# Second half-batch's scores one and a half steps later, and score products behind a whole first projection

## The chip, the cores and the metric

The kernel runs on one core of one Trainium2 chip. The time is that of one execution on the device, in microseconds, from its first instruction to its last; several runs are taken and the median is compared. Before the change it is 1001.44 us, the median of three runs from 995.87 to 1004.9.

## The reference

Three stages follow one another. All arithmetic is float32.

```python
# q, k, v: (4 batches, 8 heads, 576 positions, 64)
q_d, k_d, v_d = means over 4 neighbouring positions          # 144 positions
out_up    = repeat(softmax(q_d k_d^T / 8) v_d, 4)            # coarse attention
out_local = softmax(q k^T / 8 where |i - j| < 4) v           # band attention
x = (out_up + out_local), heads side by side                 # (2304, 512)
h = x @ w_in;  y = (h * cos(h)) @ w_out                      # 512 -> 2048 -> 512
z = ((y @ w_a) * (y @ w_b)) @ w_out2                         # 512 -> 1536 -> 512
```

## The kernel before, in words

**Attention units.** Attention is done in eight units, each half of one batch (288 positions, all 8 heads as 4 pairs). For each pair hp, `local_scores` (line 199) multiplies q and k in five windows of 64 positions, two heads each: ten products of 64x64 into one PSUM tile, which DVE reads with the mask added, reduces to a maximum (line 223) and subtracts (line 224). `down_scores` (line 226) does the coarse scores: two products of 72x144 (line 235), each reduced by DVE (line 237) and copied by ACT (line 238). All PSUM tiles of attention share the tag `att`, which has two buffers. `exps` (line 243) then does the exponentials of a unit, behind an ACT table load, and normalising, transposes, the products with v (`attend`), `combine` and the splits of x into a high and a low part (`xsplit_hi`, `xsplit_lo`) follow.

**First network.** A float32 product is made of three float32r products: high x high, high x low, low x high (`mm3`, line 420). A step g of the first network takes one block of tokens and one 128-wide slice f of the 2048: `h_mm` (line 434) is the first projection, 4 x 3 = 12 products of 128x288 into a PSUM tile with tag `h`, two buffers. `cos_a` and `cos_b` compute h*cos(h): ACT reads h (line 460), DVE reduces it (line 461), ACT takes a sine (line 465) and a square (line 468), and a last DVE instruction (line 469) multiplies with h and sets the `h` tile free. `split_hi` and `split_lo` split the result, and `back_mm` of step g - 3 does the second projection, 12 products again. Blocks 0 and 1 hold 288 tokens each and go in four runs of eight steps: block 0 with slices 0 to 7, block 1 with the same, block 0 with slices 8 to 15, block 1 with these. Block 1 needs unit 1's output, so from step 8 on.

**Weights.** Weights come by DMA as raw 64-bit words through the queue of SP and are converted: two ACT instructions (lines 104 and 107) and one of DVE (line 109) make a float32, ACT writes the high part (line 116) and POOL the low part (line 117). Two slices are wanted per step at first, so beside each step ACT also does six such instructions.

**What sets the order.** Unit 0's attention stands alone at the start. Units 1 to 7 are threaded through the steps of the first network: `unit_slots(u, g0, gl)` (line 363) spreads the tasks of unit u, each with a due time from table `T` (`T1` for unit 1), over gl steps from step g0. Slot 2g is issued in the program behind `h_mm` of step g, slot 2g+1 behind the `back_mm` of that step. For unit 1 this is `unit_slots(1, 0, FS * C["S1"])` (line 552), from step 0 over 5.6 steps; unit 2 starts at step 14. The program's order is not the engines' order: a scheduler of the framework sees priorities and dependencies and puts instructions on each engine ahead of one another where it thinks them ready, and each engine then runs its list strictly in that order. `after(ins, earlier)` (line 92) adds a dependency that only holds the order in that list and makes no semaphore wait.

In the text, a step is a step g of the first network, counted from 0.

Of the kernel before, what the change touches and what calls it, by code (L numbers as in the profile page):

```python
# [20 lines left out]
NT, DM = B * S, H * D  # L21
# [12 lines left out]
SD = S // 4  # L34
# [4 lines left out]
STARTS = ((0, 57, 114, 171, 228), (285, 342, 399, 456, 512))  # L39
BASE = (0, 284)  # L40

C = {'AHEAD': 8, 'LEAD': 4, 'NPRE': 4, 'ND': 'ddd', 'XL': 'dpp', 'SUMS0': 'dddd', 'SUMS1': 'pppp', 'GLO': 8, 'FS': 8, 'S1': 0.7, 'G2': 14, 'LC': 0, 'DM': 2, 'LAG': 3, 'NGS': 3, 'MK': 0, 'SB': 'ddd', 'NL': 'dpp', 'W0': 0, 'W1': 0, 'W2': 0, 'W3': 0, 'NWV': 3, 'NGH': 4, 'XB': 8, 'YE': 6, 'CA': 2, 'CV': 1.0, 'NE': 26, 'RA': 5, 'SA': 6, 'SD': 3, 'PA': 1, 'LAG2': 2, 'PK': 1.0, 'GE': 'ad', 'NXF': 3, 'LP': 0, 'T': {'sums': [0, 0.5, 1.0, 3.0], 'ls': [0, 0, 0, 1.5], 'ds': [1, 1.5, 3, 4], 'ex': 6, 'ln': [6.0, 9.5], 'dn': [6, 7, 9, 10], 'dt': [7, 9.5, 11, 12], 'lt': [7.5, 8.5, 12.0, 13.5], 'at': [9.5, 9.5, 13.5, 14.5], 'xh': [11.0, 12.0, 15.0, 15.5], 'xl': [12.5, 13.5, 15.5, 15.5]}, 'T1': {'sums': [0, 0, 1.0, 2.0], 'ls': [0.5, 1.5, 2.5, 3.5], 'ds': [1, 1.5, 3, 4], 'ex': 5, 'ln': [5.5, 8], 'dn': [5.0, 6.0, 8.0, 9.0], 'dt': [6.0, 7.5, 10.0, 11.0], 'lt': [7.0, 8.0, 12.0, 12.0], 'at': [9, 9, 13, 14], 'xh': [9.0, 10.0, 13.0, 14.0], 'xl': [9.5, 11, 15, 15]}}


def window_cols(half):
# [13 lines left out]
def kernel(ctx, tc, qT, kT, vw, vds, w_in, w_out, w_a, w_b, w_out2, out):  # L59
# [21 lines left out]
    def att_ps(u):  # L81
# [3 lines left out]
        turn[0] += 1  # L85
        return ps.tile([128, 512], F32, tag=tag, name="att", bufs=1 if tag.startswith("acc") else 2)

    marks = []
    gate, h_ins = {}, {}
    slots = {}  # L90

    def after(ins, earlier):
        if earlier is not None:
            tc.add_manual_dep(ins.ins, earlier.name,
                              mybir.DependencyInfo(mybir.DependencyClass.NoSync, mybir.DependencyReason.DATA),
                              reason="paces the loads")
# [102 lines left out]
    def local_scores(u, hp):  # L199
        b, half = divmod(u, 2)  # L200
        p = att_ps(u)
        pem = u < C["MK"]
        if pem:
            pe.matmul(p[:, :NW * W].rearrange("p (w k) -> p w k", k=W), identb, maskb.unsqueeze(1).to_broadcast([128, NW, W]), start=True, stop=False)
        for w, (off, _, _, _) in enumerate(window_cols(half)):
            for a in range(2):
                r = slice(64 * a, 64 * a + 64)
                pe.matmul(
                    p[r, W * w:W * w + W],
                    qt[u, hp][r, off:off + W],  # L210
                    kt[b, hp][r, BASE[half] + off:BASE[half] + off + W],
                    start=not pem, stop=True,
                )
        if hp % 2 == 0:
            smx[u, hp // 2] = at.tile([128, NW, 2, W], F32, tag="smx", name="smx", bufs=2)
        sm = smx[u, hp // 2][:, :, hp % 2]
        src = p[:, :NW * W].rearrange("p (w k) -> p w k", k=W)
        if not pem:
            dve.tensor_tensor(out=sm, in0=src, in1=mask.unsqueeze(1).to_broadcast([128, NW, W]), op=ALU.add)
            src = sm  # L220
        mx = at.tile([128, NW], F32, tag="mx", name="mx", bufs=2)
        smr[u, hp] = mx
        dve.tensor_reduce(out=mx, in_=src, axis=AX.X, op=ALU.max)
        last["sub"] = (dve if pem else pick("SB", u)).tensor_tensor(out=sm, in0=src, in1=mx.unsqueeze(2).to_broadcast([128, NW, W]), op=ALU.subtract).ins

    def down_scores(u, hp):
        b, half = divmod(u, 2)
        if hp == 0:
            smd4[u] = at.tile([QD, HP, 2, SD], F32, tag="smd", name="smd", bufs=1)
        sm = smd4[u][:, hp]  # L230
        mx = at.tile([QD, 2], F32, tag="mxd", name="mxd", bufs=2)
        p = [att_ps(u) for a in range(2)]
        for a in range(2):
            r = slice(64 * a, 64 * a + 64)
            pe.matmul(p[a][:QD, :SD], qd[u, hp][r, :], kd[b, hp][r, :], start=True, stop=True)
        for a in range(2):
            dve.tensor_reduce(out=mx[:, a:a + 1], in_=p[a][:QD, :SD], axis=AX.X, op=ALU.max)
            last["neg"] = act.activation(out=sm[:, a], in_=p[a][:QD, :SD], func=AF.Identity, bias=mx[:, a:a + 1], scale=-1.0).ins
        smd[u, hp] = sm
# [123 lines left out]
    def unit_slots(u, g0, gl):  # L363
        T = C["T"] if u > 1 else C["T1"]
        todo = []
        for hp in range(HP):
            todo += [(T["sums"][hp], down_sums, u, hp), (T["ls"][hp], local_scores, u, hp), (T["ds"][hp], down_scores, u, hp),
                     (T["dn"][hp], down_norm, u, hp), (T["dt"][hp], down_transpose, u, hp),
                     (T["at"][hp], attend, u, hp), (T["at"][hp], combine, u, hp), (T["xh"][hp], xsplit_hi, u, hp),
                     (T["xl"][hp], xsplit_lo, u, hp, pick("XL", u))]  # L370
        todo += [(T["ex"], exps, u)]
        for pr in range(HP // 2):
            todo += [(T["ln"][pr], local_norm, u, pr)] + [(T["lt"][2 * pr + i], local_transpose, u, pr, i) for i in range(2)]
        todo += [(min(T['ls'][0], T['sums'][0]) + 1, load_q, u, 3)]
        for hp in range(HP):
            todo += [(6 + hp, load_k, u + 1, hp)] + ([(6 + hp, load_q, u + 1, hp)] if hp < 3 else [])
        todo += [(15, load_v, u + 1)]
        for i in range(H):
            todo += [(i, load_vs, u, i // 2, i % 2), (i + 2, sum_vs, u, i // 2, i % 2)]
        order = [load_vs, sum_vs, load_q, load_k, down_sums, local_scores, down_scores, exps, local_norm, down_norm, local_transpose,  # L380
                 down_transpose, attend, combine, xsplit_hi, xsplit_lo, load_v]
        for t, *task in sorted(todo, key=lambda t: order.index(t[1])):
            slots.setdefault(int(2 * (g0 + t / NF * gl)), []).append(task)
# [36 lines left out]
    def mm3(ps_out, lh, ll, rh, rl, start, stop):  # L420
        i = pe.matmul(ps_out, lh, rh, start=start, stop=False)  # L421
        pe.matmul(ps_out, lh, rl, start=False, stop=False)  # L422
        pe.matmul(ps_out, ll, rh, start=False, stop=stop)  # L423
        return i

    def proj(psum, whi, wlo, u):
# [7 lines left out]
    def h_mm(g, u, f):  # L434
        hps[g] = ps.tile([128, UN1[u][1]], F32, tag="h", name="h", bufs=2)
        ins = proj(hps[g], *wts["i", f], u)
        gate.setdefault(u + 1, ins)
        h_ins[g] = ins

    def back_mm(first, last, whi, wlo, hi, lo, n=NB):  # L440
# [64 lines left out]
    if True:  # L505
# [43 lines left out]
        seq = [(i, u, f) for i, (u, f0, f1) in enumerate(blocks) for f in range(f0, f1)]  # L549
        NG = len(seq)  # L550
        slots.clear()
        unit_slots(1, 0, FS * C["S1"])
        unit_slots(2, C["G2"], 2 * NF - C["G2"])
        for u in range(3, 7):
            unit_slots(u, 2 * NF + 12 * (u - 3), 12)
# [423 lines left out]
```

## Time and profile before

| | us |
|---|---|
| three runs, median (lowest to highest) | 1001.44 (995.87 to 1004.9) |
| span of the profiled execution | 1001.5 |
| PE busy in it | 964.9 |
| DVE busy | 669.1 |
| ACT busy | 581.9 |
| POOL busy | 327.9 |

The span of the profiled execution is its own time; it differs from the median of the runs by 0.06 us. PE is TensorE, DVE VectorE, ACT ScalarE, POOL GpSimd and SP the engine that issues the DMAs. Busy time of PE is counted at whatever clock was granted at the moment: 1.2 GHz shows as a granted clock of 0.50, 2.4 GHz as 1.00, and numbers between are stretches that hold both. A PE that is busy at 0.50 does half of the work per microsecond. Instructions of the profile carry lines of the kernel before; in the changed kernel the same instructions have line numbers 1 to 4 higher.

### The profile page before, as it was taken

What the parts mean: (1) busy time and instruction counts of PE and PEld (TensorE: products, weight loads), DVE (VectorE), ACT (ScalarE), POOL (GpSimd) and SP (SyncE); (2) the same over time, 40 slices, a digit from 0 to 9 for tenths busy, and PEclk for the clock granted to TensorE, in tenths of its full rate; (3) what the DMA queues carried; (4) which work ended last, traced back from release to release, by engine and by line L of the source; (5) the groups of instructions that cost most, each with busy time, mean ns of one, the idle gap of its engine ahead of it and who ended that gap; (6) DMA issues with size and microseconds to landing.
All of it is one profiled execution on the core that took longest, in us unless ns stands there. A gap on an engine that the chain in (4) does not pass through costs nothing. (4 is left out here: it accounts for less than half of the span.)

```text
span 1001.5 us, 18883 instructions
## 1 busy us (share of the span) xinstructions
PE 964.9 (96%) x6936; PEld 917.0 (92%) x6936; DVE 669.1 (67%) x1410; ACT 581.9 (58%) x1327; POOL 327.9 (33%) x463
## 2 busy tenths in 40 slices
PE   4999999999999999999998999999999999999998
PEld 3778888989889989899997999999999999999998
DVE  7567677577777867765456567676677667676752
ACT  5589897476776848676576743444444345434321
POOL 3756752014221441101045234442043330233310
PEclk8569999999999999999999999999999999999999
DMA  8546611144555363333277983326702128734000
GB/s 277 209 137 204 196 64 32 56 141 125 167 159 165 123 183 109 115 98 103 77 240 266 333 271 97 105 70 212 250 23 63 44 82 302 225 127 129 1 32 32
DMA packets 75644, 141.28 MB, mean 141 GB/s; under 512 B 6432, under 2 KB 46624, under 8 KB 75552
## 3 DMA queue, kind: packets, MB, share of 16 engines
q1 hardware_dynamic: 75552, 140.08, 42.9%
q8 instruction: 55, 0.90, 0.4%
q14 instruction: 37, 0.30, 0.1%
HBM read 110.95 MB, written 29.10 MB: 140 GB/s over the span
## 5 line engine op out<-in xcount | busy, mean ns | idle before, releaser
L832 DVE TENSOR_TENSOR ev<-ev,z 128x384 f32<-128x384 f32 x252 | 135.4, 550 | 70.9 <-PE z L423 67.6
L421 PE MATMUL h<-xh,w 128*128 128x288 f32 (+1 forms) x448 | 148.8, 332 | 8.7 <-DVE gs L469 8.7
L421 PE MATMUL acc<-gh,w 128*128 128x288 f32 (+1 forms) x448 | 144.8, 324 | 3.0 <-DVE ev L454 1.7
L422 PE MATMUL h<-xl,w 128*128 128x288 f32 (+1 forms) x448 | 145.3, 324 | 0.0
L422 PE MATMUL acc<-gl,w 128*128 128x288 f32 (+1 forms) x448 | 142.7, 319 | 1.6 <-POOL gl L477 1.4
L423 PE MATMUL h<-xh,w 128*128 128x288 f32 (+1 forms) x448 | 144.0, 321 | 0.0
L423 PE MATMUL acc<-gh,w 128*128 128x288 f32 (+1 forms) x448 | 142.1, 317 | 0.0
L790 POOL TENSOR_TENSOR sb<-w,sb 128x256 fp32r<-128x256 f32 x96 | 75.5, 787 | 186.3 <-ACT sb L788 169.4
L421 PEld LDWEIGHTS h<-xh,w 128*128 128x128 f32 x448 | 87.2, 195 | 16.7 <-DVE gs L469 12.2
L788 ACT ACTIVATE sb<-w 128x256 fp32r<-128x256 f32 x144 | 59.9, 416 | 66.2 <-PE z L423 62.5
L422 PE MATMUL z<-xl,sb 128*128 128x384 f32 x288 | 97.0, 337 | 0.0
L421 PE MATMUL acc<-gh,wb 128*128 128x384 f32 x288 | 96.9, 337 | 0.0
L423 PE MATMUL acc<-gh,wb 128*128 128x384 f32 x288 | 96.9, 337 | 0.0
L423 PE MATMUL z<-xh,sb 128*128 128x384 f32 x288 | 96.9, 336 | 0.0
L421 PE MATMUL z<-xh,sb 128*128 128x384 f32 x288 | 96.9, 336 | 0.0
L422 PE MATMUL acc<-gl,wb 128*128 128x384 f32 x288 | 96.9, 336 | 0.0
L421 PEld LDWEIGHTS acc<-gh,w 128*128 128x128 f32 x448 | 84.8, 190 | 9.1 <-issue 2.9
L469 DVE SCALAR_TENSOR_TENSOR gs<-gs,h 128x288 f32<-128x288 f32 (+1 forms) x112 | 55.2, 493 | 56.6 <-ACT gs L468 56.3
L422 PEld LDWEIGHTS h<-xl,w 128*128 128x128 f32 x448 | 87.7, 196 | 2.3 <-issue 0.9
L790 POOL TENSOR_TENSOR sb<-ws,sb 128x256 fp32r<-128x256 f32 x72 | 54.0, 749 | 108.4 <-ACT sb L788 84.8
L423 PEld LDWEIGHTS h<-xh,w 128*128 128x128 f32 x448 | 87.8, 196 | 1.5 <-issue 0.2
L422 PEld LDWEIGHTS acc<-gl,w 128*128 128x128 f32 x448 | 85.3, 190 | 3.5 <-POOL gl L477 1.6
(138 smaller groups left out, 2302.3 us busy)
## 6 DMA issues: line engine op xcount, KB each, us to landing
wb<-wd SPq DMA_DIRECT2D x72, 512.0 KB
raw<-in_w_in_dram SPq DMA_DIRECT2D x16, 512.0 KB
raw<-in_w_out_dram SPq DMA_DIRECT2D x16, 512.0 KB
praw<-in_w_a_dram SPq DMA_DIRECT2D x12, 512.0 KB
praw<-in_w_b_dram SPq DMA_DIRECT2D x12, 512.0 KB
praw<-in_w_out_dram SPq DMA_DIRECT2D x12, 512.0 KB
wd<-praw SPq DMA_DIRECT2D x12, 512.0 KB
wd_a<-praw SPq DMA_DIRECT2D x12, 448.0 KB
```

The source lines that it names most:

```text
L421: i = pe.matmul(ps_out, lh, rh, start=start, stop=False)
L422: pe.matmul(ps_out, lh, rl, start=False, stop=False)
L423: pe.matmul(ps_out, ll, rh, start=False, stop=stop)
L469: dve.scalar_tensor_tensor(out=s, in0=s, scalar=1.0, in1=hps[g], op0=ALU.subtract, op1=ALU.mult, reverse0=True)
L788: act.activation(out=t[:, 0], in_=blk, func=AF.Copy)
L790: (dve if nst[0] % C["SD"] == 0 else pool).tensor_tensor(out=t[:, 1], in0=blk, in1=t[:, 0].bitcast(F32), op=ALU.subtract)
L832: dve.tensor_tensor(out=dst, in0=a, in1=z, op=ALU.add)
```

## The change

Two things. A start `G1` of 1.5 replaces the 0 of unit 1's slots, so that all tasks of unit 1, not only its scores, are issued one and a half steps later. And every score product, local or coarse, of any unit that is issued after the first `h_mm`, is ordered on PE behind the last product of the latest `h_mm` that was issued before it: `mm3` notes its last product, `h_mm` keeps it. A score product can no longer slip in between the twelve products of the step it is issued behind, nor ahead of them. (It can still stand among the products of a later step.)

```diff
-C = {'AHEAD': 8, 'LEAD': 4, 'NPRE': 4, ...
+C = {'G1': 1.5, 'AHEAD': 8, 'LEAD': 4, 'NPRE': 4, ...
...
+    dense = {}
     marks = []
...
             for a in range(2):
                 r = slice(64 * a, 64 * a + 64)
-                pe.matmul(
+                ins = pe.matmul(
                     p[r, W * w:W * w + W],
...
+                after(ins, dense.get("h"))
...
-            pe.matmul(p[a][:QD, :SD], qd[u, hp][r, :], kd[b, hp][r, :], start=True, stop=True)
+            ins = pe.matmul(p[a][:QD, :SD], qd[u, hp][r, :], kd[b, hp][r, :], start=True, stop=True)
+            after(ins, dense.get("h"))
...
-        pe.matmul(ps_out, ll, rh, start=False, stop=stop)
+        dense["last"] = pe.matmul(ps_out, ll, rh, start=False, stop=stop).ins
...
         gate.setdefault(u + 1, ins)
+        dense["h"] = dense["last"]
...
-        unit_slots(1, 0, FS * C["S1"])
+        unit_slots(1, C["G1"], FS * C["S1"])
```

No instruction is added or left out; the lists of the engines are put in another order, from the first projection to about step 27. The first place is PE at steps 0 and 1. In the names, `h_530` is the PSUM tile of step 0, `h_549` or `h_633` that of step 1, `h_628` that of step 2; `att<-k,q` are local and `att<-kd,qd` coarse score products of unit 1; x10 is ten products in a row. Before:

```order
L421 MATMUL h_530<-xh_393,w_476 128x288
L422 MATMUL h_530<-xl_395,w_476 128x288
L423 MATMUL h_530<-xh_393,w_476 128x288
L208 MATMUL att_560<-k_101,q_320 64x64 x3
L421 MATMUL h_530<-xh_436,w_476 128x288
L208 MATMUL att_560<-k_101,q_320 64x64 x7
L235 MATMUL att_578<-kd_153,qd_548 72x144
L422 MATMUL h_530<-xl_438,w_476 128x288
L423 MATMUL h_530<-xh_436,w_476 128x288
L421 MATMUL h_530<-xh_468,w_476 128x288
L422 MATMUL h_530<-xl_470,w_476 128x288
```

And in the changed kernel, from the middle of step 1:

```order
L424 MATMUL h_549<-xh_393,w_484 128x288
L425 MATMUL h_549<-xl_395,w_484 128x288
L426 MATMUL h_549<-xh_393,w_484 128x288
L424 MATMUL h_549<-xh_436,w_484 128x288
L425 MATMUL h_549<-xl_438,w_484 128x288
L426 MATMUL h_549<-xh_436,w_484 128x288
L424 MATMUL h_549<-xh_468,w_484 128x288
L425 MATMUL h_549<-xl_470,w_484 128x288
L426 MATMUL h_549<-xh_468,w_484 128x288
L209 MATMUL att_602<-k_101,q_320 64x64 x10
L237 MATMUL att_620<-kd_153,qd_590 72x144
L237 MATMUL att_621<-kd_153,qd_590 72x144
```

Before, the first ten local products are cut in two by step 0, and pairs 0, 1 and 2 of unit 1 have their scores among the products of steps 0 to 2. After the change the 24 products of steps 0 and 1 stand in one row, pair 0 stands behind them, pairs 1 and 2 behind step 2, and pair 3 behind step 3.

The second place is POOL at the same time, where `w_484` is the low part of the first projection's weights of step 1 and `qd` are sums of q for the coarse scores of unit 1. Before:

```order
L183 TENSOR_TENSOR qd_552<-q_363 128x72
L184 TENSOR_TENSOR qd_552<-qd_552,q_363 128x72
L185 TENSOR_TENSOR qd_552<-qd_552,q_363 128x72
L183 TENSOR_TENSOR qd_556<-q_397 128x72
L117 TENSOR_TENSOR w_484<-raw_111,w_484 128x512
```

After:

```order
L184 TENSOR_TENSOR qd_594<-q_363 128x72
L185 TENSOR_TENSOR qd_594<-qd_594,q_363 128x72
L186 TENSOR_TENSOR qd_594<-qd_594,q_363 128x72
L118 TENSOR_TENSOR w_484<-raw_111,w_484 128x512
L118 TENSOR_TENSOR w_492<-raw_117,w_492 128x512
```

The weights' low part now stands ahead of the third pair's sum, which can only be written when the coarse products of pair 0 have let go of one of the two `qd` buffers.

The third place is PE again, where the scores of unit 2 stand. Before, three pairs together at once behind the back projection of step 5:

```order
L421 MATMUL acc<-gh,w 128x288
L422 MATMUL acc<-gl,w 128x288
L423 MATMUL acc<-gh,w 128x288
L208 MATMUL att<-k,q 64x64 x30
L235 MATMUL att<-kd,qd 72x144
L421 MATMUL h<-xh,w 128x288
```

After, behind the first projection of step 14, where they are issued:

```order
L425 MATMUL h<-xl,w 128x288
L426 MATMUL h<-xh,w 128x288
L209 MATMUL att<-k,q 64x64 x20
L424 MATMUL acc<-gh,w 128x288
L425 MATMUL acc<-gl,w 128x288
L426 MATMUL acc<-gh,w 128x288
L209 MATMUL att<-k,q 64x64 x10
L424 MATMUL acc<-gh,w 128x288
```

The scheduler had pulled the first three pairs of unit 2 some seven steps ahead of their slot; the order dependency now keeps them behind step 14, together with the coarse products and, from step 16, the fourth pair, which stood there before too.

## Rows read from the trace of the kernel before

**Rows 1.** The page's 40 slices of the span: granted clock of TensorE, in tenths.

```profile
PEclk8569999999999999999999999999999999999999
```

**Rows 2.** Stretches: length, then busy us of each engine (instructions), clock, DMA share, GB/s.

```profile
36.00:63.00 27.00, 27.00 (x154) 20.65 (x151) 15.84 (x35) 17.36 (x35) 11.81 (x17) 0.50 0.55 183
75.00:110.00 35.00, 30.87 (x291) 28.84 (x291) 24.43 (x44) 31.83 (x71) 25.43 (x26) 0.93 0.57 192
110.00:165.00 55.00, 50.50 (x393) 46.78 (x392) 42.29 (x90) 49.58 (x112) 28.52 (x33) 1.00 0.28 90
```

**Rows 3.** Stretches of 2 us, PE alone: busy us (products), clock, DMA share, GB/s.

```profile
62.00:64.00 2.00, 2.00 (x12) 0.72 0.16 66
98.00:100.00 2.00, 2.00 (x10) 0.50 0.75 185
```

**Rows 4.** Timeline of PE, from step 0 on; a score product shows as two instructions.

```profile
36.05 0.61 PE L421 MATMUL h<-xh,w 128*128 128x288 f32 x1
...
41.55 0.44 PE L422 MATMUL h<-xl,w 128*128 128x288 f32 x1
41.79 0.44 PE L423 MATMUL h<-xh,w 128*128 128x288 f32 x1
...
46.38 1.33 PE L208 MATMUL att<-k,q 64*64 64x64 f32 x20
47.65 0.75 PE L235 MATMUL att<-kd,qd 64*72 64x144 f32 x2
...
49.45 0.44 PE L423 MATMUL h<-xh,w 128*128 128x288 f32 x1
...
50.50 0.61 PE L421 MATMUL h<-xh,w 128*128 128x288 f32 x1
...
60.41 0.44 PE L421 MATMUL h<-xh,w 128*128 128x288 f32 x1
...
84.85 0.29 PE L421 MATMUL h<-xh,w 128*128 128x288 f32 x1
...
86.43 0.30 PE L421 MATMUL acc<-gh,w 128*128 128x288 f32 x1
```

**Rows 5.** Timeline of ACT; in brackets its idle time before, and what ended it.

```profile
39.11 0.64 ACT L116 ACTIVATE w<-raw 128x512 fp32r<-128x512 f32 x1
42.27 0.41 ACT L460 ACTIVATE gs<-h 128x288 int32<-128x288 f32 x1 [2.51 <-PE h L423]
...
46.56 0.43 ACT L468 ACTIVATE gs<-gs 128x288 f32<-128x288 f32 x1
49.93 0.41 ACT L460 ACTIVATE gs<-h 128x288 int32<-128x288 f32 x1 [2.93 <-PE h L423]
...
60.59 1.28 ACT L246 ACT_TABLE_LOAD   x1
```

**Rows 6.** Who ACT waited for, 36 to 63 us: total us, times, longest us.

```profile
ACT gs L460 <- PE h L423: 5.4, 2, 2.9
ACT smd L238 <- DVE mxd L237: 3.8, 4, 1.0
```

**Rows 7.** Timeline of DVE, where it works on step 0 and pair 0.

```profile
37.97 1.18 DVE L361 TENSOR_TENSOR xl<-xf,xh 128x288 fp32r<-128x288 f32 x2
40.09 0.49 DVE L219 TENSOR_TENSOR smx<-att,mask 128x320 f32<-128x320 f32 x1 [0.94 <-PE att L208]
40.77 0.30 DVE L237 TENSOR_REDUCE mxd<-att 72x1 f32<-72x144 f32 x1 [0.19 <-PE att L235]
...
49.74 0.44 DVE L469 SCALAR_TENSOR_TENSOR gs<-gs,h 128x288 f32<-128x288 f32 x1
```

**Rows 8.** Timeline of POOL at the same place.

```profile
43.27 1.30 POOL L117 TENSOR_TENSOR w<-raw,w 128x512 fp32r<-128x512 f32 x1
```

**Rows 9.** Timeline of PE behind unit 2's scores, and DVE's subtractions, 86 to 130 us (count, busy, mean ns).

```profile
96.79 0.40 PE L421 MATMUL h<-xh,w 128*128 128x288 f32 x1 [2.14 <-DVE gs L469]
...
L224 DVE TENSOR_TENSOR smx<-smx,mx 128x320 f32<-128x320 f32 x4 | 3.0, 760 | 0.0
```

More of the change, by code (lines that the diff above doesn't have):

```diff
@@ L40 @@
 BASE = (0, 284)
-C = {'AHEAD': 8, 'LEAD': 4, 'NPRE': 4, 'ND': 'ddd', 'XL': 'dpp', 'SUMS0': 'dddd', 'SUMS1': 'pppp', 'GLO': 8, 'FS': 8, 'S1': 0.7, 'G2': 14, 'LC': 0, 'DM': 2, 'LAG': 3, 'NGS': 3, 'MK': 0, 'SB': 'ddd', 'NL': 'dpp', 'W0': 0, 'W1': 0, 'W2': 0, 'W3': 0, 'NWV': 3, 'NGH': 4, 'XB': 8, 'YE': 6, 'CA': 2, 'CV': 1.0, 'NE': 26, 'RA': 5, 'SA': 6, 'SD': 3, 'PA': 1, 'LAG2': 2, 'PK': 1.0, 'GE': 'ad', 'NXF': 3, 'LP': 0, 'T': {'sums': [0, 0.5, 1.0, 3.0], 'ls': [0, 0, 0, 1.5], 'ds': [1, 1.5, 3, 4], 'ex': 6, 'ln': [6.0, 9.5], 'dn': [6, 7, 9, 10], 'dt': [7, 9.5, 11, 12], 'lt': [7.5, 8.5, 12.0, 13.5], 'at': [9.5, 9.5, 13.5, 14.5], 'xh': [11.0, 12.0, 15.0, 15.5], 'xl': [12.5, 13.5, 15.5, 15.5]}, 'T1': {'sums': [0, 0, 1.0, 2.0], 'ls': [0.5, 1.5, 2.5, 3.5], 'ds': [1, 1.5, 3, 4], 'ex': 5, 'ln': [5.5, 8], 'dn': [5.0, 6.0, 8.0, 9.0], 'dt': [6.0, 7.5, 10.0, 11.0], 'lt': [7.0, 8.0, 12.0, 12.0], 'at': [9, 9, 13, 14], 'xh': [9.0, 10.0, 13.0, 14.0], 'xl': [9.5, 11, 15, 15]}}
+C = {'G1': 1.5, 'AHEAD': 8, 'LEAD': 4, 'NPRE': 4, 'ND': 'ddd', 'XL': 'dpp', 'SUMS0': 'dddd', 'SUMS1': 'pppp', 'GLO': 8, 'FS': 8, 'S1': 0.7, 'G2': 14, 'LC': 0, 'DM': 2, 'LAG': 3, 'NGS': 3, 'MK': 0, 'SB': 'ddd', 'NL': 'dpp', 'W0': 0, 'W1': 0, 'W2': 0, 'W3': 0, 'NWV': 3, 'NGH': 4, 'XB': 8, 'YE': 6, 'CA': 2, 'CV': 1.0, 'NE': 26, 'RA': 5, 'SA': 6, 'SD': 3, 'PA': 1, 'LAG2': 2, 'PK': 1.0, 'GE': 'ad', 'NXF': 3, 'LP': 0, 'T': {'sums': [0, 0.5, 1.0, 3.0], 'ls': [0, 0, 0, 1.5], 'ds': [1, 1.5, 3, 4], 'ex': 6, 'ln': [6.0, 9.5], 'dn': [6, 7, 9, 10], 'dt': [7, 9.5, 11, 12], 'lt': [7.5, 8.5, 12.0, 13.5], 'at': [9.5, 9.5, 13.5, 14.5], 'xh': [11.0, 12.0, 15.0, 15.5], 'xl': [12.5, 13.5, 15.5, 15.5]}, 'T1': {'sums': [0, 0, 1.0, 2.0], 'ls': [0.5, 1.5, 2.5, 3.5], 'ds': [1, 1.5, 3, 4], 'ex': 5, 'ln': [5.5, 8], 'dn': [5.0, 6.0, 8.0, 9.0], 'dt': [6.0, 7.5, 10.0, 11.0], 'lt': [7.0, 8.0, 12.0, 12.0], 'at': [9, 9, 13, 14], 'xh': [9.0, 10.0, 13.0, 14.0], 'xl': [9.5, 11, 15, 15]}}
 def window_cols(half):
```

## Prediction

> **What bounds the kernel now.** I read the page's slices first. TensorE has the full clock nearly everywhere; it lacks it at the start, in the first three slices of 25 us [rows 1]. So the stretches come next. From 36 us, where the first projection begins, to 63 us PE is busy for 27.00 of 27.00 us at a granted clock of 0.50, the 1.2 GHz level; ACT is busy for 17.36 of them, so ACT has 9.64 us free [rows 2]. From 75 to 165 us it is otherwise: PE is busy for 30.87 of 35 and 50.50 of 55 us at 0.93 and 1.00, and ACT for 31.83 and 49.58 [rows 2]. There both are near 90% and wait for one another in turns; neither has much to give. So in the first stretch a slow PE is the bound and ACT is kept waiting, and in the second ACT's conversions of weights and cosines weigh as much as PE's products. ACT's own waits from 36 to 63 us say so: 5.4 us in two waits for the products of a step, 3.8 us in four waits for the maxima of coarse scores, which in their turn wait for PE [rows 6].
>
> When does the clock rise? In the stretch from 62 to 64 us (0.72, so the rise is inside it) [rows 3], after the twelve products of a step that starts at 60.41 with no attention between [rows 4]. In the 24 us before, the score products of unit 1 stood among the steps, PE was as busy, and the clock stayed at 0.50.
>
> A rule of the Trainium skill bears on this: "TensorE: Matmul & The Clock Gate", Part 1, says that the chip sets this clock by how busy the PE has recently been. By busy time alone it should have risen at once; the rows above speak against so simple a reading, and if it held, the clock of the changed kernel would gain nothing from the new order (the second rival).
>
> **The change, step by step.** Nothing is added or taken away, so the cost is in who waits for whom. Products of a step start 0.24 us apart at half clock (41.55 to 41.79), so twelve take 2.88 us; at full clock twelve take 1.58 (84.85 to 86.43) [rows 4]. Ten local products take 1.33 us at half clock, one coarse product 0.75 [rows 4].
>
> *Step 0.* It starts at 36.05 as before. The low parts of x for its last two groups come from DVE at about 38.6 and 39.15 (37.97 plus 1.18 for two) [rows 7], so half of it waits there: six products to 37.5, two waits, the last one at about 39.6 to 39.85. Before, it ended at 42.23 (41.79 plus 0.44) [rows 4], as 30 score instructions stood in it. ACT reads it at 39.85 and not at 42.27 [rows 5]: **2.4 us** of waiting gone.
>
> *Step 1.* The high part of its weights is ready at 39.75 (39.11 plus 0.64) [rows 5]. The low part was made by POOL at 43.27, in 1.30 us [rows 8], behind a sum that waited for a buffer; now it stands ahead of that sum, so from 39.75 to 41.05. PE loses about 0.8 us there and then does ten products: step 1 ends at 43.5, not at 49.9 (49.45 plus 0.44) [rows 4]. ACT's second long wait, 2.93 us [rows 5], goes: its list puts the read of step 1 behind the square of step 0, and that square moves from 46.56 to about 43.5 with the read. **2.9 us**.
>
> *Scores of pair 0 and step 2.* The ten local products go from 43.6 to 44.9 and the two coarse ones to 46.3, if the clock is still low. On DVE the last instruction of step 0's cosine, which sets the `h` tile free, now stands behind the maxima of pair 0: 46.3 plus 0.30 for the maximum and 0.44 for itself gives 47.05 [rows 7]. Step 2 starts there; before at 50.50 [rows 4], so 3.4 us sooner, with 0.75 us of idle PE. ACT's split of step 0 waits for the same DVE instruction: ACT is through with the weights ahead of it at about 44.7, so a **new wait of 2.35 us** (0.9 if the clock has risen by 43.5, as pair 0's products then take half).
>
> *Clock.* From 36.05 to 43.5 there are 24 products with two gaps of about 0.8 to 0.95 us, and no attention. That is twice the row of 60.41 to 63, so I expect 1.00 somewhere from 40 to 47 us, not at 63. From then on a step is 1.58 us, and ACT finds every step, and nearly all coarse maxima, ready. I leave 1.0 us of the 3.8 us of waits for maxima.
>
> *Exponentials.* Pair 3's scores end no later than before, since steps 2 and 3 run at full clock; the table load for them, at 60.59 before [rows 5], comes 0 to 1.5 us sooner. But steps 3 and 4 have then been read and more weights converted, which before came after it. During the exponentials PE runs dry, as it did before, and I expect the clock to fall once there too.
>
> *Queues.* On SP two more loads of weights stand ahead of the load of pair 3's q, which waits for pair 0's scores; weights come sooner, and q is needed only at step 3. Nothing there ends last.
>
> *Sum.* 2.4 + 2.9 + 3.8 - 1.0 - 2.35 = 5.75 us of ACT's time, out of 9.64 that were free; with the early rise inside step 1 it is 7.2. As ACT and PE are both near 90% up to 165 us, what ACT has gained at 63 us is carried to the end: I take **6.5 us**, between the two. The least is 0 (PE only moves its idle time), the most 9.64, all that ACT had free.
>
> *Unit 2's scores.* They leave the place behind step 5, where DVE's load made PE wait 2.14 us [rows 9] and the clock fell to 0.50 (98 to 100 us) [rows 3], for steps 14 to 16. Three pairs are 3 x (0.49 + 0.49 + 0.76) = 5.2 us of DVE (mask [rows 7], maximum taken alike, subtraction [rows 9]). DVE is free for 12.7 of the 55 us from 110 to 165 [rows 2]. I take the relief and the new load as equal, zero; the bounds are the first and third rivals.
>
> The profiled execution lasts 1001.5 us, the median of runs is 1001.44; 1001.5 - 6.5 gives **995 us**.
>
> **Rivals.**
> 1. *More: the relief counts too.* With unit 2's scores gone from 88 us, the wait of 2.14 us and the low clock behind it go (ten products in 98 to 100 us [rows 3] at 0.11 us each, 1.1), and DVE takes the scores in its free time later: 995 - 3.2 = **991.8 us**. For it: DVE's 23% of free time. Against: the load stands now with the fourth pair's.
> 2. *The change doesn't do what it says: no early rise.* The two gaps, or pair 0's scores, keep the clock at 0.50 up to about 60 us. Then steps 2 to 4 and the first back projection cost 1.3 us more each, 5.2 us: 995 + 5.2 = **1000.2 us**. For it: 24 us of busy PE that did not raise it [rows 2]. Against: the row from 60.41, half as long, did [rows 3, 4].
> 3. *Slower: DVE becomes the bound at steps 14 to 16.* The 5.2 us of DVE push back the last cosine instruction of two steps; PE, which keeps its list, waits behind local products that want one of two `att` buffers, twice as long as the 2.14 us [rows 9], 4.3 us, and the clock falls for two steps of 1.3 us: 5.2 + 4.3 + 2.6 = 12.1, so 995 + 12.1 = **1007 us**. It decides if DVE's free time there is less than about half of its 12.7 us share, that is if this place costs over 6.5 us. The wait at 96.79 speaks for it, the full clock and 23% free time against. [...]
>
> **Chances.** Forecast 0.53 (990 to 999 by itself), rival 1 0.22, rival 2 0.15, rival 3 0.10. The runs of before lie between 995.87 and 1004.9, so a shift of under 1%, 10 us, can't be told well from none. Faster than 991.4: nearly half of rival 1 and a quarter of the forecast, 0.23. Slower than 1011.5: a third of rival 3, and a little, 0.05. Within 1%: 0.72. The range: from rival 1 less the 5.6 us by which the lowest run is under the median, about **986**, to rival 2 with the 3.5 us by which the highest is over it, about **1003.5**; most of rival 3 is left out.
>
> **What would show it.** Right: the read of step 0 by ACT at 39 to 40.5 us, that of step 1 at about 44, step 2's first product at 45.5 to 47.5; a granted clock of 1.00 before 47 us; ACT's waits between 36 and 63 us at 3 to 4.5 us, not 9.2; the first projection of step 8, at 96.79 before, 5 to 8 us sooner, and that distance still there at 165 us. Wrong: a clock of 0.50 at 50 us (rival 2); a distance that is there at 110 us and lost by 165 us (rival 3, with DVE over 95% busy at steps 14 to 16); or a table load for the exponentials that comes later than 62 us.

## The result: slower by 0.64%, and the profile after

| | us |
|---|---|
| changed kernel, median of 11 runs (lowest to highest) | 1006.05 (1003.02 to 1009.09) |
| kernel before, median of 11 runs (lowest to highest) | 998.03 (995.18 to 1004.9) |
| ratio of the two kernels, with its 95% interval | 1.0064 (1.0041 to 1.0087) |
| profiled execution of the changed kernel: its time, its span | 1006.91, 1005.1 |

About 6.4 us were lost by the ratio, where 6.5 were expected to be gained; the time lies outside the range. (The medians differ by 8.0 us and the means by 7.2; the text goes by the ratios and their intervals.) In every run the time is about 1.8 us above the span, so the profiled run of before (span 1001.5) took about 1003.3, which is 2 to 5 us more than the medians of before in the batches here (998.0 to 1001.3). The prediction set that span against the median as if they were one thing.

Lines of the changed kernel are 1 to 4 higher: ACT reads a step at L464 (L460 before), the products are L424 to L426, the last instruction of the cosine is L473, DVE's copy out of the accumulators L458.

The early part came much as forecast. This is ACT's timeline of the changed kernel at steps 0, 1, 2 (start, duration, in brackets the idle time before):

```profile
39.66 0.41 ACT L464 ACTIVATE gs<-h 128x288 int32<-128x288 f32 x1 [0.50 <-PE h L426]
43.72 0.39 ACT L464 ACTIVATE gs<-h 128x288 int32<-128x288 f32 x1
50.48 0.41 ACT L464 ACTIVATE gs<-h 128x288 int32<-128x288 f32 x1 [1.54 <-PE h L426]
```

Against [rows 5], steps 0 and 1 are read 2.6 and 6.2 us sooner; of the two waits of 2.51 and 2.93 us, 0.50 is left at step 0 and nothing at step 1. ACT's waits from 36 to 63 us, against [rows 6]:

```profile
ACT gs L464 <- PE h L426: 2.3, 3, 1.5
ACT gh L477 <- DVE gs L473: 2.0, 1, 2.0
ACT smd L241 <- DVE mxd L240: 1.0, 3, 0.4
```

The clock rose later than forecast: PE's timeline has products 0.24 us apart up to the rows below, the first at 0.13.

```profile
53.09 0.40 PE L424 MATMUL h<-xh,w 128*128 128x288 f32 x1
53.34 0.30 PE L425 MATMUL h<-xl,w 128*128 128x288 f32 x1
```

And the exponentials came later, not sooner. This is their table load on ACT in the changed kernel:

```profile
62.67 1.28 ACT L249 ACT_TABLE_LOAD   x1
```

Before it was at 60.59 [rows 5]. It stands behind unit 1's last coarse scores, whose products start on PE at 61.17 us here and at 59.08 before.

Then the stretches (length, busy us of PE, PEld, DVE, ACT and POOL, clock, DMA share, GB/s) of the changed kernel:

```profile
36.00:62.00 26.00, 24.30 (x171) 19.45 (x170) 15.73 (x36) 20.49 (x43) 16.58 (x20) 0.68 0.47 146
62.00:80.00 18.00, 11.96 (x106) 10.50 (x105) 12.42 (x29) 14.24 (x41) 11.80 (x10) 0.72 0.28 101
80.00:109.00 29.00, 25.68 (x228) 24.07 (x227) 17.85 (x30) 27.60 (x63) 19.57 (x22) 1.00 0.51 168
109.00:118.00 9.00, 4.81 (x25) 4.58 (x25) 2.94 (x7) 4.22 (x9) 5.50 (x8) 0.81 0.74 208
118.00:165.00 47.00, 43.00 (x374) 39.91 (x373) 39.25 (x89) 42.05 (x92) 21.77 (x21) 1.00 0.22 71
```

ACT is free (length less its busy time) for 5.51 us up to 62, where before had 9.64 up to 63 in [rows 2]; for 3.76 during the exponentials (62 to 80); and for 4.78 of the 9 us from 109 to 118. In that third place PE, DVE and ACT are busy for 4.81, 2.94 and 4.22 of the 9 us. Who waits there (total us, times, longest):

```profile
PE acc L424 <- DVE ev L458: 4.2, 1, 4.2
DVE ev L458 <- DMA y_part<-ev: 4.1, 1, 4.1
ACT gh L477 <- DVE gs L473: 3.0, 1, 3.0
```

It is the end of block 0's first half: four accumulators are copied out, two by ACT and two by DVE, into a ring of three buffers (tag `xf`), and each copy is stored to `y_part`. The fourth copy needs the buffer of a store. First who SP's queue waits for from 100 to 109 us (total us, times, longest), then the queue itself, and DVE and PE behind it:

```profile
SPq L164 <- POOL vd L177: 3.4, 2, 1.8
```

```profile
106.90 0.32 SPq L164 DMA_DIRECT2D vs<-in_vds_dram  x1
107.31 1.30 SPq L101 DMA_DIRECT2D raw<-in_w_in_dram  x1
108.66 1.46 SPq L459 DMA_DIRECT2D y_part<-ev  x3
```

```profile
113.19 0.46 DVE L458 COPY ev<-acc 128x288 f32<-128x288 f32 x1 [4.12 <-DMA y_part<-ev]
```

```profile
113.70 0.40 PE L424 MATMUL acc<-gh,w 128*128 128x288 f32 x1 [4.19 <-DVE ev L458]
...
114.28 0.44 PE L425 MATMUL acc<-gl,w 128*128 128x288 f32 x1
```

ACT's copies start at 105.34, but the stores are issued only from 108.66 on, behind two loads, the first of which waits for POOL; PE stands still for 4.19 us and then runs at half clock (0.44 us a product) up to 117.4. From the first store's issue to the fourth copy it is 4.5 us, as in the profile of before (109.22 to 113.68); what is new is that the first store goes out 3.3 us after ACT's first copy begins and not 1.0.

A fourth place is unit 2's scores, now behind the first projection of step 14. ACT reads steps 14, 15 and 16 at:

```profile
121.35 0.41 ACT L464 ACTIVATE gs<-h 128x288 int32<-128x288 f32 x1
126.97 0.40 ACT L464 ACTIVATE gs<-h 128x288 int32<-128x288 f32 x1
133.60 0.40 ACT L464 ACTIVATE gs<-h 128x288 int32<-128x288 f32 x1
```

and DVE has next to no free time there, 0.6 us from step 14 to step 16 (121.35 to 133.60). Two stretches in which it has none (the columns as above):

```profile
125.00:128.00 3.00, 3.00 (x24) 2.64 (x23) 3.00 (x8) 3.00 (x7) 0.29 (x1) 1.00 0.29 92
131.00:137.00 6.00, 5.46 (x39) 4.67 (x40) 6.00 (x14) 5.21 (x13) 1.77 (x2) 1.00 0.47 155
```

### The profile page after: what moved, and what is told of

It reads as the page before. It is cut to its first block, busy times and chain, and to the rows that moved or that the text cites. A ratio compares the mean times of both kernels' runs of the same rounds, so it can differ in the third digit from the quotient of the medians.

```text
span 1005.1 us, 18871 instructions
## 1 busy us (share of the span) xinstructions
PE 960.9 (96%) x6936; PEld 914.6 (91%) x6936; DVE 665.3 (66%) x1410; ACT 583.4 (58%) x1327; POOL 331.1 (33%) x463
## 5 line engine op out<-in xcount | busy, mean ns | idle before, releaser
L424 PE MATMUL h<-xh,w 128*128 128x288 f32 (+1 forms) x448 | 148.9, 332 | 10.2 <-DVE gs L473 10.0
L424 PE MATMUL acc<-gh,w 128*128 128x288 f32 (+1 forms) x448 | 144.7, 323 | 5.0 <-DVE ev L458 5.0
L426 PE MATMUL h<-xh,w 128*128 128x288 f32 (+1 forms) x448 | 144.6, 323 | 0.6 <-POOL w L118 0.5
L426 PE MATMUL acc<-gh,w 128*128 128x288 f32 (+1 forms) x448 | 141.5, 316 | 0.0
L424 PEld LDWEIGHTS h<-xh,w 128*128 128x128 f32 x448 | 87.6, 196 | 17.7 <-DVE gs L473 13.8
L426 PE MATMUL acc<-gh,wb 128*128 128x384 f32 x288 | 97.0, 337 | 0.0
L426 PE MATMUL z<-xh,sb 128*128 128x384 f32 x288 | 96.9, 336 | 0.0
L424 PE MATMUL z<-xh,sb 128*128 128x384 f32 x288 | 96.9, 336 | 0.0
L424 PE MATMUL acc<-gh,wb 128*128 128x384 f32 x288 | 96.8, 336 | 0.0
L424 PEld LDWEIGHTS acc<-gh,w 128*128 128x128 f32 x448 | 84.3, 188 | 10.5 <-DVE ev L458 5.5
L473 DVE SCALAR_TENSOR_TENSOR gs<-gs,h 128x288 f32<-128x288 f32 (+1 forms) x112 | 55.2, 493 | 57.0 <-ACT gs L472 56.8
L426 PEld LDWEIGHTS h<-xh,w 128*128 128x128 f32 x448 | 87.9, 196 | 3.2 <-POOL w L118 1.3
L426 PEld LDWEIGHTS acc<-gh,w 128*128 128x128 f32 x448 | 84.5, 189 | 2.1 <-issue 1.0
```

The source lines that it names most:

```text
L426: dense["last"] = pe.matmul(ps_out, ll, rh, start=False, stop=stop).ins
L473: dve.scalar_tensor_tensor(out=s, in0=s, scalar=1.0, in1=hps[g], op0=ALU.subtract, op1=ALU.mult, reverse0=True)
```

## The experiments

Theory A: the loss is the stores' wait. B: it is unit 2's pile of scores at steps 14 to 16. C: unit 1's later start makes PE run dry during the exponentials, and the low clock behind that takes the gain back. D came later. Ratios are to the runs of before in the same batch; each has 12 runs against 29 or 35, unless said otherwise.

**1. Two of block 0's first four stores from ACT's queue.**

```diff
-            sp.dma_start(out=dst[:, m, s:s + n], in_=t)
+            (act if dst is y_part and s == 0 and m % 2 == 0 else sp).dma_start(out=dst[:, m, s:s + n], in_=t)
```

> The changed kernel, but the two stores of block 0's first half that ACT copies out of PSUM are issued by ACT's own queue, right behind the copy, and not by SP, where they stand behind loads. Theory A (what is gained early is lost where block 0's first half is written out: the fourth copy needs the buffer whose store is stuck in SP's queue, PE waits 4.2 us for it and the clock falls): that wait shrinks to under 2 us, the clock stays at 1.00 around 110 us, and the time comes 3 to 5 us under the changed kernel, about 1002 us. Theory B (unit 2's scores at steps 14 to 16 load DVE): the scores still stand there, so the time stays at 1005 to 1007 us. Theory C (unit 1's later start makes PE run dry during the exponentials): also unchanged.

1002.91 us, 1.0036 (1.0017 to 1.0056): about 2.8 us of the 6.4 are gone. The two stores are issued at once from ACT's own queue, and DVE's second copy, the last of the four, starts 5.9 us sooner:

```profile
104.64 0.90 ACTq L459 DMA_DIRECT2D y_part<-ev  x2
```

```profile
107.28 0.45 DVE L458 COPY ev<-acc 128x288 f32<-128x288 f32 x1
```

The rest of what came free here is lost at unit 2's scores: step 14 to step 16 takes 14.76 us (115.39 to 130.15), against 12.25 in the changed kernel. So A and B both hold, and in this profile the first wait had hidden part of the second loss.

**2. The dependency on unit 1 alone.** The later start is kept.

```diff
-                after(ins, dense.get("h"))
+                after(ins, dense.get("h") if u == 1 else None)
```

> The changed kernel with the new order dependency on unit 1's score products alone; unit 2's go back to steps 8 and 9. Theory A: the write-out of block 0 comes a little later, the wait for its fourth copy goes from 4.2 to 1 to 3 us, time 1001 to 1004 us. Theory B: the loss goes whole and the early gain stays, 994 to 997 us. Theory C: unchanged, 1005 to 1007 us.

1000.49 us, 0.9991 (0.9969 to 1.0013). The whole loss is gone, as B has it and A and C don't; but the early gain that B left standing (994 to 997 us) isn't there either. Unit 2's first 30 local products stand behind the first projections of steps 7 and 8 (behind step 6's in before, behind step 14's in the changed kernel); SP issues three of the four stores from 105.37 on, and the fourth copy waits 0.36 us:

```profile
104.56 0.32 SPq L164 DMA_DIRECT2D vs<-in_vds_dram  x1
104.94 0.34 SPq L101 DMA_DIRECT2D raw<-in_w_in_dram  x1
105.37 1.37 SPq L459 DMA_DIRECT2D y_part<-ev  x3
```

**3. The later start alone**, with no dependency.

> Only the later start of unit 1 (1.5 steps), no order dependency on score products. Theory A: the clock rises late again, near 60 us, so the write-out of block 0 comes late too and waits little for its store: 998 to 1001 us. Theory B: no pile of unit 2's scores, so as before or better, 995 to 998 us. Theory C: the loss is all here, 1004 to 1007 us.

1004.81 us, 1.0050 (1.0026 to 1.0073). That is what theory C expected, and neither A nor B; but experiment 2 has the same start and no loss, so what the start costs hangs on how unit 1's scores are ordered (Open). Its profile was of its fastest run (1001.19); even there step 5 to step 7 takes 13.9 us, against about 10.2 before.

**4. The dependency alone**: `'G1': 0`.

> Only the order dependency of score products, unit 1 starting at step 0 as before. Theory A: the write-out of block 0 is ahead of that of the kernel before by less than in the changed kernel and waits for its store 1 to 3 us: 1000 to 1003 us. Theory B: unit 2's scores are at steps 14 to 16, so the whole loss: 1004 to 1007 us. Theory C: no loss, 994 to 998 us.

1003.93 us, 1.0039 (1.0020 to 1.0058), just under B's range and above A's. The fourth copy waits for its store here too, 3.0 us, so that wait doesn't need the later start. But here the stores go out at 104.36, 2.2 us after ACT's first copy begins, and the fourth copy starts 6.0 us later and not 4.5, so the late issue is only a part of this wait.

**5. The dependency on units 2 to 7 alone**: `'G1': 0`, and `dense.get("h") if u > 1 else None`.

> The kernel before with the new dependency on the score products of units 2 to 7 alone: unit 1 starts and runs as before. Theory B (from step 14 on, unit 2's scores come in a pile behind whole first projections, and VectorE is late with them): the distance to before is within 1 us up to step 13, then 2 to 5 us are lost at steps 14 to 16, and the median is 1002 to 1004 against some 1000 of before. Rival (what was lost there is lost because TensorE was late already from block 0, so unit 2's move alone costs nothing): no step loses over 1 us, median within 1 us of before.

1002.55 us, 1.0029 (1.0007 to 1.0051). Its profile was of its fastest run (997.30; five of the twelve took 1006 to 1010, and no profile shows those). Step 14 to step 16 takes 12.98 us (112.87 to 125.85) and DVE is busy for 11.99 of the 12 us from 119 to 131; with unit 2 free (experiment 2) the same steps take 9.62 and DVE is busy for 9.64 of those 12 us. Theory B, at its lower end. The wait for the store is 0.4 us here; one of over 2 us showed only in two profiles, of the changed kernel and of experiment 4, in which unit 1's scores were held back too.

**6. Dry stretches filled, in the changed kernel**, here in `local_transpose`, and 11 such products in `attend`.

```diff
+        for _ in range(16 if (u, pr, part) == (1, 0, 0) else 0):
+            pe.matmul(p[:, :128], ident, ident, start=True, stop=True)
         for i, s in enumerate(sl):
```

> The changed kernel with 16 additional products of the identity by itself (128 columns, results overwritten) ahead of unit 1's first transposes and 11 ahead of its first attention products, the two places where TensorE ran dry for 3.30 and 2.37 us. Theory C (the cost of the later start is the low clock that follows these dry stretches): the granted clock stays at 1.00 from 62 to 80 us where it was 0.50 from 70 to 80, and of the changed kernel's 1006 us at least 3 go: 1003 or less. Rival (the exponentials on ScalarE bound these steps, whatever the clock): the clock is up and the time stays within 1 us of 1006, or the products delay the transposes and it is longer.

1007.27 us, 1.0064 (1.0037 to 1.0091). Inconclusive: the second group's tile was not free until ACT had made its copy, so its products waited 2.62 us for the very thing they were to bridge, and then took 5.06 us at half clock. In its profile the stores' wait is 0.5 us (step 12 to 13 takes 3.50 us), and another of 4.9 us on ACT at 250 us is there (last section).

**7. The same in the kernel before**, with 4 and 2 products.

> The kernel before with 4 such products ahead of unit 1's first transposes (0.89 us idle there in its profile) and 2 ahead of its first attention products (0.49 us). Theory C: a low stretch at 66 to 77 us costs the kernel before 3 to 4 us in most of its runs (its runs with a mean clock of 0.997 and more took 995.1 to 996, those at 0.99 took 999 to 1006), so the median falls from 1000 to 996 to 998. Rival (that difference comes from elsewhere): median within 1 us of before.

999.26 us, 0.9979 (0.9956 to 1.0001): no gain that is certain, and the products still went 0.24 us apart from 73.0 to 77.9.

**8. The kernel before, profiled again.**

> The kernel before, unchanged, profiled a second time. Theory D (whether the clock is low from 15 to 63 us is drawn anew in each run and is not a matter of the order of the products): the clock is 1.00 from 36 to 62 us, as in the four experiments before, ScalarE's reads of steps 0 to 2 come 3 to 7 us sooner than in the first profile, and the run still takes 995 to 1004. Rival (the small score products among the first products of a step hold the clock down, as the prediction had it): 0.50 at 36 to 62 us again.

1002.83 us, one run. Here my expectation itself was at fault. It says of the experiments before it that the clock was 1.00 from 36 to 62 us; I had read the column of the granted clock. Their products in that stretch stand 0.24 us apart at first, as at half clock. I go by the products from here on (last section). In this run they reached 0.13 at 46.35, fell back at 48.97 and were up for good at 59.18: neither theory.

**9. Unit 1's dependency alone, dry stretches filled better.** Experiment 2 with 16 such products as in 6, and 11 into unused columns behind the transposes of unit 1's second pair.

> The changed kernel with the dependency on unit 1 alone (as in the second experiment, 1000.5 us), and with products of the identity by itself that fill TensorE's dry stretches: 16 ahead of unit 1's first transposes (3.29 us idle there), and 11 behind its last transposes (2.37 us idle ahead of the attention products), into columns that nothing reads. Theory C (what unit 1's later start gains by step 2 is lost again to the low clock that follows these dry stretches): from 64 to 79 us the 128x288 products go by 0.13 us apart and not by 0.24, step 5 is read by ScalarE at 73 to 76 us and not at 78, and the median is 996 to 998. Rival (the exponentials and what VectorE and ScalarE do about them bound steps 3 to 5 at either clock): step 5 within 1 us of 78, median 1000 to 1001.

999.81 us, 0.9994 (0.9968 to 1.0021). From 62 to 80 us experiment 2 has PE busy for 12.20 of 18 us at a granted clock of 0.62; here:

```profile
62.00:80.00 18.00, 17.75 (x185) 16.65 (x186) 13.51 (x32) 16.94 (x48) 11.90 (x10) 1.00 0.33 114
```

and from 53.69 to 80 us products stand 0.24 us apart only where a row of them begins. Step 2 to step 5 takes 26.86 us, against 29.83. So C's mechanism is there and is worth 3 us between these steps; but step 5 itself is read at 77.46, within 1 us of experiment 2's 78.07 as the rival had it, by step 17 the two profiles stand level (130.53 and 130.98), and the median gains nothing that can be told. As an account of the result C falls.

**10. The whole change, unit 2 from step 9 on**: `'G2': 9`.

> The changed kernel whole, dependency and all, with unit 2's steps begun at step 9 and not 14, so that its first 30 local score products stand behind steps 10 and 11 and not behind step 15. Theory B (the loss is the pile at steps 14 to 16, where VectorE has no room): the stores' wait at 109 to 113 us is under 1 us, no step from 13 to 16 loses over 1.5 us against before's profile, median 1000 to 1002. Rival (the dependency costs by itself, since a score product behind a whole projection waits longer for VectorE wherever it stands): the loss moves to steps 10 to 13, median 1004 to 1007.

1002.15 us, 1.0012 (0.9993 to 1.0031). Each theory has half: the fourth copy waits 0.9 us for its store and PE not at all, but step 11 to step 14 takes 17.05 us (10.87 in experiment 2), with unit 2's first local products behind step 9's first projection and among step 10's. Some 3 us of that are made up by step 25 (170.60, against 164.63).

**11. The later start alone, once more.**

> The later start of unit 1 with no dependency, once more: its first profile was its fastest run (1001.2 of a median of 1004.8), so it did not show what the others lose. Theory C: in a typical run the 128x288 products go 0.24 us apart for 12 us or longer from 64 us on and again at 88 to 92 us, and the distance to before grows there by 2 to 3 us over the first profile. Rival (the 4.3 us between this and the kernel with the dependency on unit 1 is an accident of 12 runs): the median now is within 1.5 us of 1001.

1004.63 us, 1.0030 (1.0013 to 1.0048): not an accident. Products went 0.24 us apart up to 54.48 and again from 77.65 to 81.71 us; the fall at 88 to 92 us was not repeated.

**12. Experiments 1 and 2 together.**

> The later start with the dependency on unit 1 alone, and two of block 0's four first-half stores issued from ScalarE's queue. Theory A (the stores' wait is a consequence of unit 2's scores at step 14 and is gone without them): nothing to gain over the second experiment, median 1000 to 1001. Rival (0.9 us of the wait is left there and goes): 999 to 1000.

1000.66 us, 0.9991 (0.9972 to 1.0010): nothing beyond experiment 2, as theory A has it, though its profile has a wait of 1.8 us for the store. For the main verdict it is a second set of runs without unit 2's dependency.

**13 to 16. Four more looks at the kernel before.**

> The kernel before, unchanged, profiled again (first of four looks). Theory D (the run that the prediction was worked out from had a late rise of the clock and was 3 to 4 us over the median, so most of what an early rise can give, a typical run has already): in most of the four looks the 128x288 products reach 0.13 us spacing before 55 us, step 2 is read by ScalarE at 51 to 55 us and not at 57, and the later the read of step 5, the longer the run, at 995 to 1003 us. Rival (the premise held, and the gain was lost elsewhere alone): the spacing is 0.24 us up to 59 us or later in all four, step 2 is read at 56 to 58, and runs that differ by 5 us or more do so behind step 25.

> The kernel before, second look; expectations as for the first.

> The kernel before, third look; expectations as for the first.

> The kernel before, fourth look; expectations as for the first.

In us: from when on the 128x288 products are 0.13 apart, and when ACT reads a step.

| | 0.13 from | step 2 | step 5 | step 12 | step 13 | step 16 | step 25 | the run |
|---|---|---|---|---|---|---|---|---|
| before, profile of the prediction | 63.23 | 57.01 | 83.48 | 114.06 | 117.69 | 130.85 | 168.39 | about 1003.3 |
| before again (8) | 46.35, fell back to 59.18 | 54.59 | 82.21 | 112.83 | 116.41 | 129.54 | 167.32 | 1002.83 |
| look 4 (16) | 62.31 | 56.31 | 82.44 | 113.10 | 116.51 | 129.74 | 167.29 | 1002.02 |
| look 2 (14) | 52.05 | 53.65 | 80.80 | 111.39 | 114.91 | 128.22 | 165.93 | 1000.61 |
| look 1 (13) | 46.78 | 52.67 | 79.82 | 110.36 | 114.37 | 127.23 | 164.87 | 999.58 |
| look 3 (15) | 46.65 | 52.61 | 79.65 | 110.26 | 113.81 | 128.02 | 164.81 | 999.56 |
| changed | 53.34 | 50.48 | 80.12 | 110.00 | 118.18 | 133.60 | 170.76 | 1006.91 |
| 1: stores by ACT | 50.75 | 48.70 | 78.14 | 107.81 | 112.33 | 130.15 | 167.72 | 1002.74 |
| 2: unit 1 alone | 46.12 | 48.24 | 78.07 | 110.40 | 113.81 | 127.19 | 164.63 | 999.02 |
| 9: unit 1, filled | 53.69 | 50.60 | 77.46 | 109.47 | 112.79 | 126.66 | 164.71 | 1004.47 |
| 12: unit 1, stores by ACT | 52.47 | 49.72 | 79.18 | 112.85 | 116.62 | 127.85 | 165.04 | 998.80 |

Theory D holds, for about half of the profiles. In three looks of four, and in three of six profiles in all, the kernel before has its early rise already, with unit 1's scores among the products; these are the runs near the median. How many runs of before rise early is not shown; of its 110 runs in the batches, 80 took less than the 1002.02 us of look 4, the shortest run with a late rise. PE of look 3:

```profile
44.81 1.28 PE L208 MATMUL att<-k,q 64*64 64x64 f32 x20
46.02 0.46 PE L235 MATMUL att<-kd,qd 64*72 64x144 f32 x2
46.41 0.40 PE L422 MATMUL h<-xl,w 128*128 128x288 f32 x1
46.65 0.29 PE L423 MATMUL h<-xh,w 128*128 128x288 f32 x1
46.78 0.29 PE L421 MATMUL h<-xh,w 128*128 128x288 f32 x1
```

The runs with a late rise are late at step 5 and step 25 and are the longer ones (among the three late ones the order is not strict): from look 3 to the prediction's profile 3.8 us at step 5, 3.6 at step 25, some 3.7 in the time. And step 25, in look 3 and in experiment 2 (ACT):

```profile
164.81 0.41 ACT L460 ACTIVATE gs<-h 128x288 int32<-128x288 f32 x1 [0.47 <-PE h L423]
```

```profile
164.63 0.41 ACT L464 ACTIVATE gs<-h 128x288 int32<-128x288 f32 x1 [0.45 <-PE h L426]
```

No version here is surely faster than the kernel before: experiment 7 comes nearest, and its interval ends at 1.0001. What differs with unit 1's part of the change alone is the spread: the 24 runs of experiments 2 and 12 lie between 997.53 and 1001.81 us, the 110 of before between 995.07 and 1007.28.

## Why the prediction was wrong

**Steps 0 to 2 were right.** Read of step 0 at 39.66 (forecast 39 to 40.5), of step 1 at 43.72 (about 44), first product of step 2 at 46.72 (45.5 to 47.5), ACT's split of step 0 waits 2.0 us (2.35). (One reading was off, and nothing hangs on it: 22 score instructions stood in step 0 before, not 30.)

**The clock was late.** "I expect 1.00 somewhere from 40 to 47 us, not at 63": it was 53.3, so the sign set for rival 2, half clock at 50 us, was there, though not its 60 us; and ACT's waits up to 63 us were 5.5 us and not 3 to 4.5. In the eight profiles of kernels with unit 1's dependency the products were at 0.13 us for good (up to the exponentials) between 42.5 and 53.7 us; of the eight without it and without the later start, three were by 52.1 and five only between 58.0 and 63.2. So the order may make a late rise rarer, as the prediction had it, but it does not fix the time.

**The failed step, first half: the sum.** "What ACT has gained at 63 us is carried to the end: I take 6.5 us". The distance to the profile of before was 6.5 us at step 2, 3.4 at step 5. (Step 8's first product came 3.6 us sooner, at 93.23, and not 5 to 8.) Two things took it. The gain was worked out against a run whose clock rose at 63 us, while three of the six profiles of before, those near the median, have it up at 47 to 52 (experiments 13 to 15): what the early rise gives, these runs have already. And the later start makes the exponentials late. "Pair 3's scores end no later than before [...]; the table load for them [...] comes 0 to 1.5 us sooner": it came 2.1 us later, past the 62 us that the prediction set as a sign of being wrong. Against a run of before with an early rise it is 7.8 us; in look 3:

```profile
54.83 1.28 ACT L246 ACT_TABLE_LOAD   x1
```

In every profile with the later start it comes between 60.2 and 63.0 us, whenever the clock rose; in the others between 54.8 and 60.6. Behind it stand unit 1's transposes. Who waits there in the changed kernel, 64 to 74 us:

```profile
PE att L304 <- DVE sd L291: 3.3, 1, 3.3
PE att L323 <- ACT smx L306: 2.4, 1, 2.4
```

Before, these two waits were 0.89 and 0.49 us. The half clock behind them lasts to 80.6 here. What the prediction called a fall "once there too", it had not priced: filling these waits gave 3 us up to step 5 in experiment 9. Against look 3, the changed kernel is 2.1 us ahead at step 2, 0.5 behind at step 5, 0.3 ahead at step 12. Idle time of ACT was moved, as in these stretches of look 3:

```profile
36.00:62.00 26.00, 22.02 (x164) 16.85 (x162) 19.75 (x49) 19.79 (x49) 14.14 (x17) 0.95 0.59 190
62.00:80.00 18.00, 17.87 (x182) 16.47 (x181) 8.97 (x15) 15.52 (x41) 10.92 (x11) 0.69 0.18 56
109.00:118.00 9.00, 8.52 (x65) 8.27 (x64) 5.67 (x12) 8.64 (x20) 6.25 (x9) 1.00 0.61 193
```

6.21, 2.48 and 0.36 us free, against 5.51, 3.76 and 4.78 in the changed kernel. With unit 2 left alone the change measures 0.9991 (experiment 2, and 12 with two stores moved besides), and both intervals take in 1.0000: unit 1's part is worth some 1 us or nothing, and not 6.5.

**The failed step, second half: unit 2's scores.** "I take the relief and the new load as equal, zero." The load was set against DVE's 12.7 free us in the whole stretch from 110 to 165 us. Where it landed, from step 14 to step 16, DVE had 1.85 us free in the profile of before, against 5.2 us of new work:

```profile
121.44:130.85 9.41, 8.62 (x77) 7.78 (x76) 7.56 (x14) 8.37 (x22) 6.29 (x10) 1.00 0.43 143
```

Taking unit 2's dependency out of the change moves the ratio from 1.0064 to 0.9991: 7 us (5.6 by the medians). In the rows, against look 3, the changed kernel loses 4.6 us from step 12 to 13 (8.18 against 3.55) at the stores, and 1.8 from step 14 to 16 (12.25 against 10.47; the other five profiles of before take 9.1 to 9.6 there, so 2.7 to 3.1). At step 25 it is 5.95 behind. In experiment 1's profile, without the first, the second is 4.3; in experiment 6's, which also lacks it, 2.3 (12.72 us). The relief where the scores stood was small: step 7 to step 9 takes 9.47 us against 9.78.

**The third rival** had the place and the engine of one part: DVE full at steps 14 to 16 (11.65 of 12.25 us). It had chance 0.10, the price on PE was put on `att` buffers, and its landmark, a distance that is there at 110 us and lost by 165, is what the trace shows against the profile of before (4.1 us at step 12, -2.4 at step 25). That its 1007 us is close to the measured time is luck: it kept the gain of 6.5 us, which isn't there, and charged 12.1 us for unit 2's scores, which cost 7; and PE's wait of 4.2 us, nearly its 4.3, is at the stores and not at the `att` buffers. What stood in no sum or rival is the copy out of block 0, just ahead of unit 2's scores: its three buffers, and SP's queue, in which the load that waited for POOL up to 106.90 held up the stores behind it. A wait of 0.6 us stood there before.

**Open.** Whether every run of the changed kernel has the stores' wait: experiment 1 gained 2.8 us and not 4.2, experiment 6's profile lacks it, and in experiment 4's the stores themselves took 1.5 us longer, for no reason that was found. Why the later start alone costs 3 to 5 us and with unit 1's dependency nothing: both its profiles lose most against look 3 from step 5 to 7 (13.9 and 14.5 against 10.2 us). Half clock at step 5 is not enough to explain it: it lasts to 77.9 and 81.7 us there, and in experiment 12, which loses 0.4, to 79.7. And experiments 9 and 2 read step 25 at the same time and differ by 5 us in their profiled runs; a wait of PE at 254 us (below) is most of it, and its share in the medians was not measured.

## What to carry to other kernels

Free time that is averaged over a long stretch says little of the place where work lands: read the rows of that place. One profile is one run: where a gain hangs on when the clock rises or a wait falls, look at several profiles of the unchanged kernel first, and compare a span with spans and a time with times. A gain ahead of a stretch in which two engines are near 90% was not carried by itself here: follow it to the next place where something has to be free, above all copies that need a buffer whose store stands behind loads in one queue. And of work that is moved, find the new neighbours; "relief and load are equal" is a price that has to be worked out like any other.

## What the runs showed of the hardware

**The column of the granted clock can miss a change.** In experiment 9's profile it says 1.00 for 36 to 40 us (busy PE, products, clock, DMA share, GB/s), while the products go 0.24 us apart and take 0.44, as at half clock:

```profile
36.00:40.00 4.00, 3.64 (x14) 1.00 0.15 55
```

```profile
39.06 0.44 PE L431 MATMUL h<-xl,w 128*128 128x288 f32 x1
39.30 0.44 PE L432 MATMUL h<-xh,w 128*128 128x288 f32 x1
39.55 0.44 PE L430 MATMUL h<-xh,w 128*128 128x288 f32 x1
```

In look 4 it says 1.00 for 36 to 62 us, and the products stand 0.24 us apart up to 62.31. The same shape's duration is the better witness.

**The clock's rise is not fixed by the order of the products.** In six profiles of the kernel before, with one order, it came between 46 and 63 us, and in one of them the clock fell back at 48.97 and rose again at 59.18.

**A late load far from any change stopped PE for 4 us.** In experiment 9's profiled run ACT waited 5.0 us for a DMA of `praw`, and PE behind ACT for 4.24; then the half clock (busy PE, products, clock, DMA share, GB/s):

```profile
254.52 1.19 PE L209 MATMUL att<-k,q 64*64 64x64 f32 x20 [4.24 <-ACT praw L613]
```

```profile
256.00:260.00 4.00, 4.00 (x15) 0.50 0.61 234
```

Experiment 6's run shows it too (3.74 us). In the other 16 profiles ACT waits 1.8 to 4.2 us at this place as well, but PE has no such idle time.
